# Attention and routed experts in fp32 on one core: whole loads of q, k and v, a new order of the work, and copies in place of the last pair's last moves

## The chip, the core and the metric

The kernel runs on one core of one Trainium2 chip. The metric is device time in microseconds: the median of three runs was 614.49 us (614.11 to 616.44). Five engines take part: TensorE (PE), VectorE (DVE), ScalarE (ACT), GpSimd (POOL) and SyncE (SP), which only issues DMAs.

## What is computed

For 8 batches of 8 heads, 576 positions and head size 64, attention with rotary embedding; then, per batch, the 128 positions with the highest gate score go through a small expert network, and its result is added to their rows.

```python
scores = scale * np.matmul(q_rot, k_rot.transpose(0, 1, 3, 2))
scores = scores - np.max(scores, axis=-1, keepdims=True)
attn = np.exp(scores)
attn = attn / (np.sum(attn, axis=-1, keepdims=True) + 1e-09)
x = np.matmul(attn, v)                      # heads side by side: 8 x 576 x 512
scores = np.einsum('bsd,d->bs', x, w_gate)
top_idx = np.argpartition(-scores[b], capacity)[:capacity]
h = np.maximum(x[b, top_idx] @ w1, 0.0)
out[b, top_idx] = x[b, top_idx] + sigmoid(scores[b, top_idx])[:, None] * (h @ w2)
```

## The kernel before

**Pairs and units.** The 64 heads are worked in 32 pairs, four pairs to a batch. Inputs come packed by the host. For a pair, `load` brings k, q and v: k and q as two DMAs each, one for each half of the 128 partitions (line 464), v as one DMA to partitions 0 to 63 (line 456), which an ACT or POOL copy doubles into partitions 64 to 127 (line 459). `rotate` makes the rotary sums on POOL (lines 482, 484) and splits them into a high and a low part (lines 486, 487). `attend` makes nine units of 128 query rows: three PE products (line 536), the row maxima on DVE (line 557), the exponentials on ACT (line 565), and a 32 by 32 block transpose on DVE into `pt` (line 588). Units 0 to 3 go to `pt0`, units 4 to 8 to `pt1`.

**Moves.** After the block transposes, quarters of 32 partitions must change places. Half of what must move is first set aside by an ACT or POOL copy (line 594). Then `move` issues four DMAs from SBUF to SBUF (line 610): two `gone` moves, and two more that wait for the first two. Only then can `value` multiply by v (line 635; 128 columns for `pt0`, 160 for `pt1`), copy out (lines 347, 349), transpose back (line 688) and scale rows (lines 703 to 719). The row sums of unit 8 are spread over partitions by four small POOL copies (line 670).

**Routing and the expert.** After a batch's fourth pair, `route` makes gate scores (774), spreads them (784), counts for each row how many are higher (793, 801 to 807), and selects 128 rows (841, 849). POOL gathers these rows from the output in DRAM with an indirect DMA (865). PE transposes them (883), and the expert runs as PE products in chunks (911) with transposes of the hidden layer between (930). DVE adds the result (946), and POOL scatters it back (950). The expert of batch 6 is held until the end of the last batch.

**What sets the order.** Every piece is an `op` with the engines it may run on, an estimated cost, a priority key and what it needs. `Order.run` is a planner that walks through simulated time and gives each free engine the ready op with the smallest key; the engines then run that order as it stands, each strictly in order, with semaphores between them. Keys come from the table `KEY` (20000 units are a pair) plus noise drawn from `SEEDS`, one seed for each pair's stretch. Where PE has nothing to do in the plan and has lately been little busy, the planner puts in a filler: a product whose result nobody reads (line 358). `op`s that may run on two engines are given to the one that is free.

Of the kernel before, what the change touches and what calls it, by code (L numbers as in the profile page):

```python
# [19 lines left out]
P = 128  # L20
# [3 lines left out]
KEY = dict(warm=0.7, warm0=20000, warm1=1000000, dummy=430, dcols=256, ahead=12000, lag=16000, rem=400, value=10000, rows=3000, load=26000, rotate=115700, half=2500,  # L24
           gate=11700, route=58400, count=35500, select=12400, turn=17500, step=7600, kstep=2700, hold=3,
           vcopy=3000, lift=range(9), lifted=740, patience=900, over=300, near=-300, swap=6000, vsplit=9, vstep=0, recip=6000, pool_lo=1, esplit=2, t_most=4)


SEEDS = (85, 648, 427, 874, 17, 496, 720, 7, 849, 752, 45, 62, 610, 72, 955, 819, 905, 1, 133, 973, 819, 418, 418, 526,
         36, 895, 308, 381, 162, 522, 372, 129, 880)  # L30
# [14 lines left out]
class Order:  # L45
# [33 lines left out]
    def run(self):  # L79
# [59 lines left out]
        while events:  # L139
# [3 lines left out]
            moved = True  # L143
            while moved:
                moved = False
                for e in names:
# [126 lines left out]
def attention_moe_kernel(ctx: ExitStack, tc: tile.TileContext, q, k, v, gate, w1, w2, rope, outs, shape, cap):  # L273
# [69 lines left out]
    LOAD, VALUES, WEIGHTS, STORE = {"SP": (540, 1850)}, {"SP": (500, 2050)}, {"SP": (520, 1400)}, {"SP": (600, 2200)}  # L343
# [104 lines left out]
    def load(pi, names="kqv", after=()):  # L448
# [3 lines left out]
        for i, (n, src, tiles) in enumerate((("k", k, k_ins), ("q", q, q_ins), ("v", v, vts))):  # L452
            if n in names:
                use = uses[n] = tiles.next()
                if n == "v":
                    o = op(VALUES, lambda src=src, use=use: nc.sync.dma_start(use.tile[0:64], src[b, j]), key + i,
                           use.before + list(after), size=1450)
                    y = op({"ACT": act(2 * (NB // 2) * D), "POOL": pool_copy(2 * (NB // 2) * D)},
                           lambda e, use=use: (nc.gpsimd.tensor_copy if e == "POOL" else nc.scalar.copy)(use.tile[64:P], use.tile[0:64]),
                           key + KEY["vcopy"], [o])  # L460
                    got[n] += [o, y]
                for h in range(2 if n != "v" else 0):
                    hp = slice(64 * h, 64 * h + 64)
                    o = op(LOAD, lambda src=src, use=use, hp=hp: nc.sync.dma_start(use.tile[hp], src[b, j][hp]), key + i,
                           use.before + list(after), size=1500)
                    got[n].append(o)
                use.by(*got[n])
# [44 lines left out]
    def attend(pi):  # L512
# [36 lines left out]
        def softmax(u, key, o, b):  # L549
# [12 lines left out]
            m = op({"DVE": (KEY["lifted"], KEY["lifted"] + 131) if lift else (665, 796)}, most, key,  # L562
                   [o] + nm.before + (into.before if lift else []), b, urgent=True)
            x = op({"ACT": (728, 838)},
# [12 lines left out]
        def turn(u, key):  # L577
# [19 lines left out]
            area[c].by(o, y), side_[c].by(y)  # L597
            return [o, y]

        def move(c, key, turns):  # L600
# [15 lines left out]
            turns = sum(turns, [])  # L616
            gone = {g: part(g, two[e, 1], two[o_, 0], turns) for g, (e, o_) in up.items()}
# [8 lines left out]
        def value(c, key):  # L626
            acc, ot = Bank("s"), ots[c].next()

            def products(m0, m1):
                for m in range(m0, m1):  # L630
                    for h in range(2):
                        for g in range(2):
# [4 lines left out]
                                vt.tile[gp_, h, (m - 1) % 2 * NT + (m - 1) // 2 if m else 2 * NT, :],  # L637
# [26 lines left out]
        def reciprocals(key):  # L664

            def spread():
                for h in range(2):
                    for a in range(2):
                        at_ = 64 * a + 32 * h
                        nc.gpsimd.tensor_copy(su[32 * a:32 * a + 32, 8 + h, 0:1], su[at_:at_ + 32, 10, 0:1])  # L670
# [5 lines left out]
            sp = op({"POOL": (870, 945)}, spread, key, exps[8])  # L676
# [87 lines left out]
    def route(b):  # L764
        base = at(NP * b + NP - 1, 1.0) + KEY["route"]
        last = b == B - 1
        gp, done, stored, rs = gates.pop(b)
# [11 lines left out]
        after = key + (0 if last else KEY["count"])  # L779
# [328 lines left out]
```

## Time and profile before

| | us |
|---|---|
| median of three runs (range) | 614.49 (614.11 to 616.44) |
| the profiled execution | 613.23 |
| its span, first to last instruction | 611.4 |
| around the span | 1.8 |
| PE, DVE, ACT, POOL busy | 547.9, 496.5, 459.1, 458.3 |

The profile is of one execution. Busy time is the sum of the instructions' spans on an engine; PE's is modelled, since matmuls are pipelined, and it holds the fillers too. An idle time is put down to what ended it. In the chain of waits, the last instruction is followed back, step by step, to what released it.

### The profile page before, as it was taken

The numbers are of one execution on the slowest core, as the hardware profiler recorded it, in microseconds if no ns is written. First come the engines' busy times: TensorE is split into PE (matmuls) and PEld (weight loads), VectorE is DVE, ScalarE is ACT, GpSimd is POOL, SyncE is SP. The second block draws the span as 40 slices with busy tenths as digits, with TensorE's granted clock in tenths as the row PEclk, the third lists the DMA queues.
The fourth block names the chain that finished last, engine by engine and source line by source line (L and its number), as shares of the span: only waits on it lengthen the run. The fifth ranks groups of instructions, "written<-read, shape, count | busy, mean of one in ns | idle before, by whom it ended". The sixth has DMA issues, their size and how long they took to land.

```text
span 611.4 us, 19675 instructions
## 1 busy us (share of the span) xinstructions
PE 547.9 (90%) x7570; PEld 451.5 (74%) x7570; DVE 496.5 (81%) x1248; ACT 459.1 (75%) x1201; POOL 458.3 (75%) x479
## 2 busy tenths in 40 slices
PE   0887989996999998999989999899989999899996
PEld 0675767785887787788868787778878887688874
DVE  4978878895899999898989889889988999788221
ACT  2768899896788888788788868878789877776411
POOL 1889999997888788898878788788898698622110
PEclk9988999999899999999989999999999999899999
DMA  8599999889688698979887787877888776626410
GB/s 204 120 221 223 215 247 229 205 201 240 137 183 206 167 229 199 229 171 221 197 231 162 158 233 177 201 167 210 197 232 193 180 198 152 178 65 156 116 35 17
DMA packets 55166, 111.59 MB, mean 183 GB/s; under 512 B 7840, under 2 KB 37536, under 8 KB 55072
## 3 DMA queue, kind: packets, MB, share of 16 engines
q1 hardware_dynamic: 53648, 105.42, 72.0%
q0 software_dynamic: 1280, 4.20, 2.4%
q8 instruction: 59, 0.97, 0.7%
q10 hardware_dynamic: 144, 0.72, 0.4%
q14 instruction: 35, 0.29, 0.2%
HBM read 56.30 MB, written 11.53 MB: 111 GB/s over the span
## 4 chain that ended last, share of the span: by engine, by line
PE 33%; DMA 26%; POOL 14%; issue 10%; DVE 7%; ACT 6%; SPq 3%; POOLq 0%; DVEq 0%; ACTq 0%
DMA pt<-pt 11%; PE ps L635 11%; PE ps L911 9%; PE ps L536 9%; DMA xe<-out_dram,idx 6%; POOL turned L484 3%; DVE pab L557 3%; DMA vt<-v_dram 3%; ACT pab L565 2%; PE ps L688 2%; DVE pt L588 2%; POOL q_in L482 2%; DMA h<-w_dram 2%; POOL w L977 2%; POOL k_in L482 2%
## 5 line engine op out<-in xcount | busy, mean ns | idle before, releaser
L565 ACT ACTIVATE pab<-pab,nm 128x576 f32<-128x576 f32 x256 | 196.6, 770 | 34.5 <-DVE pab L557 33.4
L557 DVE TENSOR_SCALAR_CACHE_REDUCE pab<-ps 128x576 f32<-128x576 f32 x256 | 181.5, 745 | 35.7 <-PE ps L536 30.5
L588 DVE STREAM_TRANSPOSE pt<-pab 128x576 f32<-128x576 f32 x256 | 188.6, 760 | 21.4 <-ACT pab L565 20.9
L635 PE MATMUL ps<-pt,vt 64*64 64x128 f32 (+1 forms) x4608 | 165.6, 291 | 8.4 <-DMA pt<-pt 2.6
L635 PEld LDWEIGHTS ps<-pt,vt 64*64 64x64 f32 x4608 | 146.2, 136 | 25.0 <-issue 8.9
L536 PE MATMUL ps<-kh,qh 64*128 64x288 f32 (+1 forms) x576 | 89.7, 351 | 22.7 <-ACT qh L486 15.1
L482 POOL TENSOR_TENSOR q_in<-q_in,tabs 128x1280 f32<-128x1280 f32 x31 | 91.1, 2940 | 22.2 <-DMA q_in<-q_dram 21.9
L594 ACT COPY pt<-pt 128x288 f32<-128x288 f32 x223 | 88.6, 429 | 23.3 <-DMA pt<-pt 7.8
L536 PEld LDWEIGHTS ps<-kh,qh 64*128 64x128 f32 (+1 forms) x576 | 51.2, 190 | 59.6 <-issue 19.6
L482 POOL TENSOR_TENSOR k_in<-k_in,tabs 128x1152 f32<-128x1152 f32 x31 | 82.7, 2666 | 2.4 <-DMA k_in<-k_dram 2.2
L536 PE MATMUL ps<-kh,ql 64*128 64x288 f32 (+1 forms) x576 | 71.7, 299 | 2.7 <-POOL ql L487 2.6
L536 PE MATMUL ps<-kl,qh 64*128 64x288 f32 (+1 forms) x576 | 70.9, 296 | 0.0
L688 PE MATMUL ps<-turner,ot 128*128 128x136 f32 x320 | 52.4, 295 | 8.0 <-ACT ot L347 7.1
L358 PE MATMUL ps<-tabs,turner 128*128 128x256 f32 x202 | 56.3, 402 | 1.3 <-DVE pab L557 0.9
L536 PEld LDWEIGHTS ps<-kh,ql 64*128 64x128 f32 (+1 forms) x576 | 53.9, 190 | 3.6 <-POOL ql L487 3.0
L688 PEld LDWEIGHTS ps<-turner,ot 128*128 128x128 f32 x320 | 42.7, 191 | 16.7 <-ACT ot L347 11.0
L536 PEld LDWEIGHTS ps<-kl,qh 64*128 64x128 f32 (+1 forms) x576 | 54.0, 190 | 0.0
L487 POOL TENSOR_TENSOR ql<-turned,qh 128x640 fp32r<-128x640 f32 x31 | 48.4, 1562 | 6.3 <-ACT qh L486 5.3
L911 PE MATMUL ps<-w,ht 128*128 128x512 f32 x192 | 51.6, 408 | 0.0
L911 PE MATMUL ps<-w,xt 128*128 128x512 f32 x192 | 51.3, 407 | 0.0
L594 POOL COPY pt<-pt 128x288 f32<-128x288 f32 x65 | 27.3, 427 | 29.1 <-DVE pt L588 13.5
L484 POOL TENSOR_TENSOR turned<-q_in 128x640 f32<-128x640 f32 x31 | 48.3, 1558 | 1.1
(104 smaller groups left out, 769.1 us busy)
## 6 DMA issues: line engine op xcount, KB each, us to landing
pt<-pt SPq DMA_DIRECT2D x128, 180.0 KB
q_in<-q_dram SPq DMA_DIRECT2D x64, 320.0 KB
k_in<-k_dram SPq DMA_DIRECT2D x64, 288.0 KB
pt<-pt SPq DMA_DIRECT2D x128, 144.0 KB
vt<-v_dram SPq DMA_DIRECT2D x32, 288.0 KB
out_dram<-x SPq DMA_DIRECT2D x16, 512.0 KB
xe<-w_dram SPq DMA_DIRECT2D x8, 256.0 KB
h<-w_dram SPq DMA_DIRECT2D x8, 256.0 KB
```

Of the source, the lines that this page charges most:

```text
L358: nc.tensor.matmul(bank_of(b)[:, 0:KEY["dcols"]], ident, tabs[:, 0, 0:KEY["dcols"]], start=True, stop=True)
L482: m = op(time(2 * n), lambda: e.tensor_tensor(x[:, :, c0:c1], x[:, :, c0:c1], tab[:, :, c0:c1], op=ALU.mult), key, got)
L484: y = op(time(n), lambda: e.tensor_tensor(sum_[:, c0:c1], x[:, 0, c0:c1], x[:, 1, c0:c1], op=ALU.add), key, [m] + sum_use.before)
L487: d = op(time(n), lambda: e.tensor_tensor(lu.tile[:, c0:c1], sum_[:, c0:c1], hu.tile[:, c0:c1].bitcast(F32), op=ALU.subtract), base, [c] + ...
L536: nc.tensor.matmul(bank_of(bs[i])[:, n, 0:HALF], lt, rt, start=start, stop=stop)
L557: nc.vector.tensor_scalar(halves, bank_of(b)[:, :, 0:HALF], -1.0, None, op0=ALU.mult, op1=ALU.min, accum_out=nm.tile[:, u:u + 1])
L565: lambda: nc.scalar.activation(halves, halves if lift else bank_of(b)[:, :, 0:HALF], AF.Exp, bias=nm.tile[:, u:u + 1], scale=-1.0 if lift ...
L588: nc.vector.transpose(into, src.rearrange("p (m w j) -> p m w j", w=2, j=32))
L594: (nc.gpsimd.tensor_copy if e == "POOL" else nc.scalar.copy)(apart(c)[:, to * L:to * L + L], two)
L635: nc.tensor.matmul(bank_of(acc)[64 * h:64 * h + 64, g, c0:c0 + 32 * n], vt.tile[gp_, h, (m - 1) % 2 * NT + (m - 1) // 2 if m else 2 * NT, ...
L688: nc.tensor.matmul(bank_of(b)[:, W * i:W * i + W], ot.tile[:, i * P:i * P + P], turner, start=True, stop=True)
L911: nc.tensor.matmul(bank_of(bank), lhs.tile[:, a, c * P:c * P + P], w[w_][:, c, fs], start=(c == 0 and i == 0), stop=(c == n - 1 and i == 2))
```

## The change

- `load`: k and q are one DMA each over 128 partitions. v is repacked by the host so that one DMA brings 576 elements to each of 128 partitions, and two copies of 64 partitions by 576 elements put each half beside the other; `value` picks its operand accordingly.
- `move` and `turn`: for the `pt1` side of the last pair, the four DMAs are left out. Instead each of the five block transposes is followed by four copies of 32 partitions by 288 elements on ACT or POOL.
- the spread of unit 8's row sums may also run on ACT.
- the planner: an op on PE that needs only another op on PE is ready as soon as PE is free, not when the first one's result has landed; the expert's products are cut into chunks of one (`esplit` 1, before 2), so that a chunk is three matmuls.
- the keys, seeds and some estimated costs are new; batch 6 has its own keys for counting, selecting and turning.

```diff
-           gate=11700, route=58400, count=35500, select=12400, turn=17500, step=7600, kstep=2700, hold=3,
+           gate=10237, route=58400, count=31062, select=10850, turn=21875, step=7600, count_=20000, select_=3000, turn_=78750, step_=8550, last_step=1750, kstep=2700, hold=3,
...
-                        n.ready = max(n.ready, o.end + self.SEM)
+                        behind = e == "PE" and "PE" in n.engines
+                        n.ready = max(n.ready, free[e] if behind else o.end + self.SEM)
...
-                    o = op(VALUES, lambda src=src, use=use: nc.sync.dma_start(use.tile[0:64], src[b, j]), key + i,
-                    y = op({"ACT": act(2 * (NB // 2) * D), "POOL": pool_copy(2 * (NB // 2) * D)},
+                    o = op(VALUES, lambda src=src, use=use: nc.sync.dma_start(use.tile[:, 0], src[b, j]), key + i,
+                    for h in range(2):
+                        mine, there = slice(64 * h, 64 * h + 64), slice(64 - 64 * h, 128 - 64 * h)
+                        got[n].append(op({"ACT": act((NB // 2) * D), "POOL": pool_copy((NB // 2) * D)},
+                                             use.tile[mine, 1], use.tile[there, 0]), key + KEY["vcopy"], [o]))
-                for h in range(2 if n != "v" else 0):
-                    o = op(LOAD, lambda src=src, use=use, hp=hp: nc.sync.dma_start(use.tile[hp], src[b, j][hp]), key + i,
+                    got[n].append(op(LOAD, lambda src=src, use=use: nc.sync.dma_start(use.tile, src[b, j]), key + i,
...
+            if not c or pi < n_pairs - 1:
+                return [o, y]
+            for g in (0, 2):
+                e, o_ = slice(32 * g, 32 * g + 32), slice(32 * g + 32, 32 * g + 64)
+                needs = [o, y]
+                for out, in_ in ((two[e], one[o_]), (one[o_], apart(c)[e, to * L:to * L + L])):
+                    needs = [op({"ACT": act(L, 30), "POOL": pool_copy(L)},
...
+            if c and pi == n_pairs - 1:
+                return
...
-            sp = op({"POOL": (870, 945)}, spread, key, exps[8])
+            sp = op({"ACT": (340, 440), "POOL": (870, 945)}, spread, key, exps[8])
```

The order that comes out differs on every engine. Three places follow; the number behind a tile's name is its buffer's.

**PE, batch 4, from the selection to the transposes of the gathered rows.** L849 is the last selection product, L883 the transposes of the gathered rows; L536 are score products, L635 the products with v, L688 transposes back, L358 fillers. Before:

```order
L849 MATMUL ps<-tok_114,more 128x5
L635 MATMUL ps<-pt_91,vt_86 64x128 x36
L358 MATMUL ps<-tabs,turner 128x256
L536 MATMUL ps<-kh_79,qh_83 128x288 x4
L536 MATMUL ps<-kl_81,qh_83 128x288 x4
L536 MATMUL ps<-kh_79,ql_85 128x288 x4
L688 MATMUL ps<-turner,ot_93 128x136 x2
L358 MATMUL ps<-tabs,turner 128x256 x2
L536 MATMUL ps<-kh_79,qh_83 128x288 x4
L536 MATMUL ps<-kl_81,qh_83 128x288 x4
L536 MATMUL ps<-kh_79,ql_85 128x288 x4
L883 MATMUL ps<-turner,xe_109 128x128 x4
```

Now, with other line numbers (L897 are the transposes of the gathered rows); ahead of these rows and behind the selection stand two transposes back and a block of 36 products with v from `pt1`:

```order
L537 MATMUL ps<-kh_79,qh_83 128x288 x4
L537 MATMUL ps<-kl_81,qh_83 128x288 x4
L537 MATMUL ps<-kh_79,ql_85 128x288 x4
L537 MATMUL ps<-kh_79,qh_83 128x288 x2
L537 MATMUL ps<-kl_81,qh_83 128x288 x2
L537 MATMUL ps<-kh_79,ql_85 128x288 x2
L701 MATMUL ps<-turner,ot_94 128x136 x3
L537 MATMUL ps<-kh_79,qh_83 128x288 x4
L537 MATMUL ps<-kl_81,qh_83 128x288 x4
L537 MATMUL ps<-kh_79,ql_85 128x288 x4
L648 MATMUL ps<-pt_91,vt_86 64x128 x36
L897 MATMUL ps<-turner,xe_109 128x128 x4
```

Between the selection and these transposes there now stand two blocks of products with v instead of one, thirty score matmuls instead of twenty-four, and no filler instead of three.

**POOL, the end of the last pair.** L950 is the scatter of batch 5's expert, L865 the gather for batch 6, L594 the copies aside. Before:

```order
L594 COPY pt_92<-pt_92 128x288 x3
L594 COPY pt_91<-pt_91 128x288 x3
L594 COPY pt_92<-pt_92 128x288 x2
L950 DMA out_dram<-xe_109,idx_113 576x512
L864 CAST idx_112<-gg_116 128x1
L865 DMA xe_109<-out_dram,idx_112 128x512
```

Now (L606 are the new copies, L964 the scatter, L879 the gather):

```order
L595 COPY pt_92<-pt_92 128x288
L606 COPY pt_92<-pt_92 32x288 x5
L595 COPY pt_92<-pt_92 128x288
L606 COPY pt_92<-pt_92 32x288 x2
L964 DMA out_dram<-xe_109,idx_113 576x512
L606 COPY pt_92<-pt_92 32x288 x8
L878 CAST idx_112<-gg_116 128x1
L879 DMA xe_109<-out_dram,idx_112 128x512
```

Fifteen of the twenty new copies are POOL's, eight of them behind the scatter and ahead of the gather; five are ACT's. On SP the last four moves of `pt_92` are gone.

**PE, the last expert (batch 7), from its first product to its second.** L911 are the expert's products, L930 transposes of the hidden layer. Before:

```order
L911 MATMUL ps<-w_0_118,xt_106 128x512 x2
L911 MATMUL ps<-w_1_119,xt_106 128x512
L911 MATMUL ps<-w_0_118,xt_106 128x512
L930 MATMUL ps<-turner,h_108 128x128 x8
L358 MATMUL ps<-tabs,turner 128x256 x2
L911 MATMUL ps<-w_0_120,ht_107 128x512
```

Now (L925 the products, L944 the transposes):

```order
L944 MATMUL ps<-turner,h_108 128x128 x4
L925 MATMUL ps<-w_0_118,xt_106 128x512
L925 MATMUL ps<-w_1_119,xt_106 128x512
L925 MATMUL ps<-w_0_118,xt_106 128x512 x2
L925 MATMUL ps<-w_1_119,xt_106 128x512
L925 MATMUL ps<-w_0_118,xt_106 128x512
L925 MATMUL ps<-w_0_120,ht_107 128x512
L925 MATMUL ps<-w_1_121,ht_107 128x512
L925 MATMUL ps<-w_0_120,ht_107 128x512
L944 MATMUL ps<-turner,h_108 128x128 x4
L925 MATMUL ps<-w_0_120,ht_107 128x512
```

The first four transposes now stand after 18 of the 24 products of the first layer, and three products of the second layer stand ahead of the last four transposes. The six last products of batch 6's expert now stand behind the transposes of batch 7's gathered rows, where they stood ahead of them.

## Rows read from the trace of the kernel before

**Rows 1.** The page: TensorE's and the other engines' busy time, and the clock.

```profile
PE 547.9 (90%) x7570; PEld 451.5 (74%) x7570; DVE 496.5 (81%) x1248; ACT 459.1 (75%) x1201; POOL 458.3 (75%) x479
...
core 0: 611.4 us, clock 0.980
```

**Rows 2.** The page: the chain that ended last, shares of the span by engine.

```profile
PE 33%; DMA 26%; POOL 14%; issue 10%; DVE 7%; ACT 6%; SPq 3%; POOLq 0%; DVEq 0%; ACTq 0%
```

**Rows 3.** Stretches: us, busy us by engine, granted clock, DMA share, GB/s.

```profile
40.00:140.00 100.00, 89.77 (x1293) 73.27 (x1290) 85.39 (x210) 88.82 (x235) 96.56 (x90) 0.98 0.93 219
85.00:515.00 430.00, 400.43 (x5817) 332.11 (x5818) 378.89 (x951) 353.03 (x925) 366.00 (x368) 0.98 0.82 197
```

**Rows 4.** Waits over the whole span: total us, times, longest us.

```profile
PE ps L883 <- DMA xe<-out_dram,idx: 13.8, 6, 4.1
...
POOL sums L670 <- DMA xe<-out_dram,idx: 8.3, 3, 3.9
```

**Rows 5.** Instructions in time: PE's transposes of gathered rows, batches 0, 1 and 5.

```profile
150.88 1.12 PE L883 MATMUL ps<-turner,xe 128*128 128x128 f32 x4 [4.08 <-DMA xe<-out_dram,idx]
...
250.76 0.66 PE L883 MATMUL ps<-turner,xe 128*128 128x128 f32 x4 [1.05 <-DMA xe<-out_dram,idx]
...
524.18 0.66 PE L883 MATMUL ps<-turner,xe 128*128 128x128 f32 x4 [2.77 <-DMA xe<-out_dram,idx]
```

**Rows 6.** Stretches behind three of these transposes, columns as in rows 3.

```profile
151.00:158.00 7.00, 7.00 (x89) 5.93 (x90) 4.19 (x10) 3.11 (x7) 5.13 (x6) 0.58 0.37 82
317.50:321.00 3.50, 3.47 (x15) 2.63 (x17) 0.89 (x4) 2.32 (x6) 1.90 (x7) 0.53 0.84 216
524.00:531.00 7.00, 6.82 (x94) 5.83 (x95) 4.17 (x12) 5.48 (x14) 5.52 (x9) 0.76 0.46 138
```

**Rows 7.** Groups of instructions (count, busy us, mean ns, idle before): the fillers.

```profile
L358 PE MATMUL ps<-tabs,turner 128*128 128x256 f32 x202 | 56.3, 402 | 1.3 <-DVE pab L557 0.9 <-DMA pt<-pt 0.4
```

**Rows 8.** Instructions in time: PE's two last blocks with v, two fillers.

```profile
566.60 2.20 PE L635 MATMUL ps<-pt,vt 64*64 64x128 f32 x72
...
569.86 1.03 PE L358 MATMUL ps<-tabs,turner 128*128 128x256 f32 x4
571.22 3.12 PE L635 MATMUL ps<-pt,vt 64*64 64x160 f32 x72 [0.33 <-issue]
```

**Rows 9.** Stretches near the start, columns as in rows 3.

```profile
3.00:5.00 2.00, 0.00 (x0) 0.00 (x0) 0.12 (x5) 0.00 (x0) 0.00 (x0) 1.00 1.06 312
5.00:12.00 7.00, 0.00 (x0) 0.00 (x0) 2.11 (x2) 0.66 (x1) 0.00 (x0) 1.00 1.00 215
17.00:18.00 1.00, 1.00 (x12) 1.00 (x12) 0.73 (x2) 0.00 (x0) 0.48 (x1) 1.00 0.83 271
```

**Rows 10.** The chain in order of time: first and last of six loads, one unit pair's scores.

```profile
1.47 7.57 DMA k_in<-k_dram
...
391.23 0.99 PE ps L536 x12
...
481.08 7.27 DMA q_in<-q_dram
```

**Rows 11.** Groups of instructions: the copies that the change splits, moves or resembles.

```profile
L459 ACT COPY vt<-vt 64x1152 f32<-64x1152 f32 x24 | 27.7, 1153 | 9.0 <-DMA vt<-v_dram 8.5
L486 ACT CAST kh<-turned 128x576 fp32r<-128x576 f32 x32 | 21.4, 670 | 14.1 <-DVE turned L484 8.8 <-POOL turned L484 4.6 <-PE ps L536 0.6
L594 POOL COPY pt<-pt 128x288 f32<-128x288 f32 x65 | 27.3, 427 | 29.1 <-DVE pt L588 13.5 <-DMA pt<-pt 10.7 <-DVE rs L673 4.0
L705 ACT COPY gp<-ps 128x4 f32<-128x4 f32 (+1 forms) x26 | 4.4, 170 | 0.0
L670 POOL COPY sums<-sums 32x1 f32<-32x1 f32 x128 | 22.8, 178 | 19.9 <-DMA xe<-out_dram,idx 8.3 <-ACT pr L565 7.7
L793 DVE SCALAR_TENSOR_TENSOR more<-ps,sc,above 128x320 bf16<-128x320 f32 (+4 forms) x40 | 20.0, 535 | 1.0 <-PE ps L784 1.0
```

**Rows 12.** Instructions in time: the last pair's last maximum and copy aside, the last expert.

```profile
560.85 0.09 DVE L557 DVE_READ_ACCUMULATOR pab<-ps 128x1 f32 x1
...
564.03 0.43 ACT L594 COPY pt<-pt 128x288 f32<-128x288 f32 x1 [0.83 <-DVE xe L946]
...
591.62 6.12 PE L911 MATMUL ps<-w,xt 128*128 128x512 f32 x24
...
597.58 0.60 PE L930 MATMUL ps<-turner,h 128*128 128x128 f32 x4
...
600.10 5.94 PE L911 MATMUL ps<-w,ht 128*128 128x512 f32 x24
```

**Rows 13.** DMA issues: gathers and scatters, median us from issue to landing.

```profile
xe<-out_dram,idx POOLq DMA_INDIRECT x7, 6.5
out_dram<-xe,idx POOLq DMA_INDIRECT x7, 3.2
```

More of the change, by code (lines that the diff above doesn't have):

```diff
@@ L560, in most @@
                     nc.vector.tensor_reduce(nm.tile[:, u:u + 1], bank_of(b)[:, :, 0:HALF], axis=AX.XY, op=ALU.max, negate=True)
-            m = op({"DVE": (KEY["lifted"], KEY["lifted"] + 131) if lift else (665, 796)}, most, key,
+            m = op({"DVE": (KEY["lifted"], KEY["lifted"] + 75) if lift else (665, 796)}, most, key,
                    [o] + nm.before + (into.before if lift else []), b, urgent=True)
-            x = op({"ACT": (728, 838)},
+            x = op({"ACT": (768, 870) if lift else (728, 838)},
                    lambda: nc.scalar.activation(
@@ L597, in turn @@
             area[c].by(o, y), side_[c].by(y)
+            if not c or pi < n_pairs - 1:
[5 more added lines that the diff above has]
+                    needs = [op({"ACT": act(L, 30), "POOL": pool_copy(L)},
+                                lambda e, out=out, in_=in_: (nc.gpsimd.tensor_copy if e == "POOL" else nc.scalar.copy)(out, in_),
+                                key, needs)]
+                    area[c].by(*needs), side_[c].by(*needs), moved[c].extend(needs)
             return [o, y]
@@ L664, in reciprocals, with spread @@
         def reciprocals(key):
-            def spread():
+            def spread(e):
                 for h in range(2):
@@ L669, in spread @@
                         at_ = 64 * a + 32 * h
-                        nc.gpsimd.tensor_copy(su[32 * a:32 * a + 32, 8 + h, 0:1], su[at_:at_ + 32, 10, 0:1])
+                        (nc.gpsimd.tensor_copy if e == "POOL" else nc.scalar.copy)(su[32 * a:32 * a + 32, 8 + h, 0:1], su[at_:at_ + 32, 10, 0:1])
             def f():
@@ L766, in route @@
         last = b == B - 1
+        K = {n: KEY[n + "_" * (b == B - 2)] for n in ("count", "select", "turn", "step")}
         gp, done, stored, rs = gates.pop(b)
@@ L778, in route @@
         split = splits(sc, s, key)
-        after = key + (0 if last else KEY["count"])
+        after = key + (0 if last else K["count"])
         scores = lambda t: bank_of(bs).rearrange("p n c -> p (n c)")[0:P if t < NT else REM, t * P:S]
@@ L810, in route @@
         sc.by(s, o, *counts), mores.by(co), cnt.by(*counts, co)
-        return [chosen(b, r0, base + (0 if last else KEY["count"] + KEY["select"]), bc, co, stored, split, last)
+        return [chosen(b, r0, base + (0 if last else K["count"] + K["select"]), bc, co, stored, split, last, K)
                 for r0 in range(0, cap, P)]
@@ L827, in splits, with chosen @@
         return tk, o
-    def chosen(b, r0, key, bc, co, stored, split, last):
+    def chosen(b, r0, key, bc, co, stored, split, last, K):
         n = min(P, cap - r0)
@@ L860, in index @@
                 nc.vector.memset(xe.tile, 0.0)
-        ix = op({"DVE": dve(2, 2, 600.0 * (n < P))}, index, key, [w] + xe.before + gg.before, bp)
+        ix = op({"DVE": dve(2, 2, 600.0 * (n < P))}, index, key, [w] + (xe.before if n < P else []) + gg.before, bp)
         def rows_in():
@@ L871, in chosen, with experts_of @@
         idx.by(ga)
[L872 to L874 removed]
+        return lambda hold: experts_of(b, n, key, last, K, ga, ix, idx, xe, gg, hold)
+    def experts_of(b, n, key, last, K, ga, ix, idx, xe, gg, hold):
         xt, ht = xts.next(), hts.next()
         g = gg.tile
[L877 to L878 removed]
+        step = KEY["last_step"] if last else K["step"]
+        key += 0 if last else K["turn"]
         bx = Bank("t")
```

28 lines of the change are left out of this document (11 added, 17 removed).

## The prediction

> **What bounds the kernel now.** I read the busy shares first. PE is busy for 547.9 of 611.4 us, DVE for 496.5, ACT for 459.1, POOL for 458.3 [rows 1]: no engine is full, and PE's number holds 202 filler records, 56.3 us [rows 7], that compute nothing. The reader should see that the useful work of PE is 547.9 - 56.3 = 491.6 us, and that DVE has as much. The chain of waits says the same: PE is a third of it, DMAs are 26% [rows 2], so the end is set by a relay in which each engine in turn is late. In the middle stretch, from 85 to 515 us, PE is busy 93%, DVE 88%, POOL 85%, ACT 82% [rows 3]. Only the early stretch, in which the expert's weights are loaded too, is close to full somewhere: POOL 97%, DMA share 0.93 from 40 to 140 us [rows 3].
>
> So what counts is where the fixed orders make an engine stand in front of something late. The list of waits names one such place plainly: PE stands before the transposes of the gathered rows (L883) for 13.8 us in six batches, 4.1 us at worst [rows 4, 5]. The median gather takes 6.5 us from issue to landing [rows 13]. [...]
>
> **Part 1, the new order around the gathers.** In batches 0, 2, 3, 4 and 5 the old order puts one block of products with v between the selection and L883, the new one two. A block lasts 2.2 to 3.1 us [rows 8]; thirty score matmuls stand where 24 did in batch 4 (0.99 us for twelve [rows 10]), and three fillers, half of 1.03 us each [rows 8], are gone. In batch 4 the second block is of the longer kind, so the work that covers the gather grows by about 3.1 + 0.5 - 1.5 = 2.1 us, and by three transposes back. Batch 1 goes the other way: two blocks before and after, but twelve score matmuls fewer, so its wait of 1.05 us [rows 5] may grow by 1 us. Upper bound of the gain: 13.8 - 1.05 = 12.7 us of waiting and 6.3 us of clock, 19 us. Lower bound: nothing, if the other engines have used the pause to catch up. A second bound comes from the orders: the new one has 64 fillers, the old one 101, and a filler stands only where the plan had nothing for PE. At 56.3 / 101 = 0.56 us each [rows 7] the 37 fewer are 20.6 us. Both ends agree on some 20 us, and I take somewhat under half, **-9 us**, since DVE at 88% [rows 3] has only an eighth of its time to give.
>
> POOL also stops at a gather: a row-sum copy waits until the DMA lands, 8.3 us in three batches [rows 4]. In the new order such a wait still stands behind each gather or scatter (behind batch 3's gather it stands before a v copy). I count no gain here.
>
> **Part 2, whole loads.** Sixty-four issues fall away on SP, which costs nothing to the end by itself, as the moves behind them mostly wait for data. The bytes are the same. Near the start 312 GB/s flow while the 128-partition table is in flight and 215 while mainly halves are [rows 9]; but for one microsecond, with only the two halves of q in flight, 271 [rows 9]. Six loads are on the chain, from 7.57 us for the first k to 7.27 us for a late q, 35 us in all [rows 10]. If all sped up as 215 to 312, they would be 31% shorter: -11 us, one end. The other end is 0, since a chain that loses a load finds the next wait. By the nearest row, 271 to 312, it is 13% of 35 = 4.6 us; I take **-3 us**, the first load's part included.
>
> [...]
>
> v's copy is split. One ACT copy of 1152 elements takes 1.153 us, an ACT cast of 576 elements 0.670 [rows 11]; two are 1.34 us, 0.19 more, but they may run on two engines and start after a shorter load. I take 0.
>
> **Part 3, row sums on ACT.** By the order, 84 of the 128 small copies move from POOL to ACT. The smallest ACT copy takes 0.170 us [rows 11], so ACT gets 14.3 us, and 15.0 us leave POOL (0.178 each [rows 11]). With v's copies (45 x 0.670 - 27.7 = 2.5) and nine copies aside or moves (3.9 at POOL's 0.427 [rows 11]) ACT has 20.7 us more. The cover is ACT's idle time, 430 - 353 = 77 us in the middle stretch [rows 3]. If that cover is gone, all 20.7 us are paid. I take **+1 us**.
>
> **Part 4, the last pair's moves.** Now the last copy aside ends at 564.46 [rows 12], and the last block with v starts at 571.22 [rows 8]: 6.8 us for four moves in two steps. After it, each transposed unit is followed by four copies, 0.43 us each [rows 11]. Even if POOL did all four of the last unit in a row, that is 1.7 us: up to 5.1 us gained. Two things take some back. On DVE five counting operations for batch 6, 0.535 us on average [rows 11], now stand between the last maxima and the last two transposes: 2.7 us, partly where DVE would wait for ACT anyway. And on POOL eight of the copies stand behind batch 5's scatter, and the second of them waits for its landing, 3.2 us [rows 13]. The scatter's sum stands earlier on DVE than before, ahead of the last maxima, so the landing should be over in time. If not, the gain is about 0. I take **-3 us**.
>
> **Part 5, the last expert.** The first layer's products end at 591.62 + 6.12 = 597.74, the second layer's start at 600.10 [rows 12]: 2.36 us, of which two sets of transposes need 1.2. In the new order six products of the first layer and three of the second fill these gaps. **-1 us**, with bounds 0 and -1.2 here, and up to 1 us more because batch 6's last six products cover the conversion of batch 7's rows.
>
> **The sum.** -9 - 3 + 1 - 3 - 1 = -15 us. The profiled execution took 613.23 us (span 611.4 and 1.8 around it), so 598.2; it lies 1.26 us under the median of the runs, so on that scale I say **599 us**.
>
> **Rivals.**
>
> *Another engine keeps the pace.* PE no longer waits for gathers, but DVE, at 88%, and the relay through ACT do not deliver more scores or exponentials, and PE's pause only moves to L536 or L635. For it: the middle stretch has no single bound [rows 3]. Against: three of the waits cost the clock as well [rows 6]. Part 1 is then 0 and the sum -6: 608.5 us.
>
> *The waits go in full.* Part 1 is worth its 19 us and loads half of their upper end, 5.5 us: -19 - 5.5 - 3 - 1 = -28.5, 586 us.
>
> *ACT becomes late.* The spread of row sums stands in ACT's strict queue behind the exponential of unit 8, and the next exponentials stand behind it. If these copies are on the path of each pair, as when ACT is past about 95% in a stretch (it has 89% from 40 to 140 us [rows 3]), half to all of the 20.7 us is paid, and part 1 does not show: +10.4 or +20.7, less 7 for parts 2, 4 and 5, so +3 to +14 and in the middle 613.2 + 8.5 + 1.3 = 623 us, slower than before.
>
> *The clock falls instead.* Where fillers went, PE may pause more. Each fall costs 1.6 to 2.9 us [rows 6]. If the waits at the gathers stay and every batch has two more such falls of 1.6 us, that is 26 us against the -7 of parts 2, 4 and 5 (and +1 for ACT): about 633 us; with one in each batch, 13 us, 620. It decides once falls number more than four beyond today's. [...]
>
> **How the numbers follow.** The forecast (592 to 606 by its bounds) has a chance of 0.60, another engine keeping the pace 0.20 (its range 605 to 614), the waits going in full 0.08, ACT late 0.06, the clock 0.06. A measurement here can tell about 0.5%, 3 us, from no change: below 611.4 is faster, above 617.6 slower. Faster holds the forecast, the full case and most of the second: 0.60 + 0.08 + 0.13 = 0.81. Same gets the rest of the second and a little of the slower cases, 0.09; slower 0.10. The range leaves out about 2 in 10: the slower cases above, half of the full case below: 588 to 613.
>
> **What would show it.** [...] Wrong: PE waiting as long at the gather, or for maxima in its place; ACT's idle share vanishing with DVE waiting for it; POOL's new copies standing idle before the scatter's landing; more clock falls than now.

## The result and the profile after

The changed kernel takes **586.16 us** (median of four runs, 585.07 to 593.77), the kernel before 615.47 beside it (614.11 to 616.59): a ratio of 0.955, 95% interval 0.947 to 0.964. The sign is as forecast, the time is not: 599 was said, with a range of 588 to 613. The profiled execution took 585.07 us, its span is 583.3.

The page of the changed kernel: busy times, one DMA queue, and the chain's shares by engine.

```profile
PE 523.4 (90%) x7496; PEld 434.2 (74%) x7496; DVE 495.5 (85%) x1242; ACT 477.9 (82%) x1318; POOL 452.9 (78%) x417
...
q1 hardware_dynamic: 53968, 104.67, 65.4%
...
DMA 28%; ACT 22%; POOL 17%; PE 10%; issue 10%; DVE 9%; SPq 2%; POOLq 0%; ACTq 0%; DVEq 0%
```

Beside [rows 1, 2]: PE's share of the chain fell from 33% to 10%, and ACT's rose from 6% to 22%. ACT has 18.8 us more work, nearly the 20.7 of part 3, and the end came sooner all the same. The kernel before has this row for the same queue, which carries all loads and moves (the last number is the time that its packets took, as a share of the 16 DMA engines' span):

```profile
q1 hardware_dynamic: 53648, 105.42, 72.0%
```

72.0% of 611.4 us is 440 us on each of the 16 engines; 65.4% of 583.3 is 381. The bytes are within 1%. So **59 us of DMA time are gone, and the bytes are not**. This row of before was not among those that the prediction was built on, and it should have been.

The waits of the changed kernel over the whole span, columns as in [rows 4]:

```profile
DVE pt L589 <- ACT pab L566: 33.2, 47, 2.0
POOL q_in L483 <- DMA q_in<-q_dram: 23.2, 17, 4.4
...
ACT pab L566 <- DVE pab L558: 7.0, 17, 1.2
DVE pab L558 <- PE ps L537: 6.1, 7, 3.6
...
PE ps L897 <- DMA xe<-out_dram,idx: 0.9, 1, 0.9
...
POOL sums L683 <- DMA out_dram<-xe,idx: 0.4, 1, 0.4
```

PE's wait for the gather was 13.8 us [rows 4] and is 0.9. The kernel before has these two rows:

```profile
DVE pab L557 <- PE ps L536: 30.5, 26, 5.4
...
DVE pt L588 <- ACT pab L565: 20.9, 31, 2.4
```

DVE's wait for scores is down from 30.5 us in 26 places to 6.1 in 7: PE is hardly late any more. DVE's wait for ACT's exponentials is up, from 20.9 to 33.2. The stretches, columns as in [rows 3], and the fillers:

```profile
3.00:5.00 2.00, 0.00 (x0) 0.00 (x0) 0.12 (x5) 0.00 (x0) 0.00 (x0) 1.00 0.98 376
5.00:12.00 7.00, 0.00 (x0) 0.00 (x0) 4.56 (x6) 1.34 (x2) 2.02 (x2) 1.00 0.76 291
40.00:140.00 100.00, 89.59 (x1331) 74.37 (x1329) 86.64 (x214) 93.25 (x253) 92.66 (x66) 0.97 0.80 225
85.00:515.00 430.00, 402.99 (x6062) 334.30 (x6061) 391.57 (x985) 383.81 (x1069) 368.48 (x325) 1.00 0.76 206
```

```profile
L359 PE MATMUL ps<-tabs,turner 128*128 128x256 f32 x128 | 35.7, 403 | 2.6 <-POOL pt L595 1.4 <-ACT gp L718 1.2
```

The start runs at 376 and 291 GB/s, where it was 312 and 215 [rows 9], and from 5 to 12 us with a DMA share of 0.76 instead of 1.00. The DMA share from 85 to 515 us is 0.76 (0.82 in [rows 3]) at more GB/s, the granted clock there 1.00 instead of 0.98, and 128 filler records are left of 202.

**Where the time went.** Each pair has one sum for its reciprocals, on DVE (line 673 before, 686 now). Pairs 21 and 22 in the kernel before, then in the changed one; PE's transposes of batch 3's gathered rows stand between:

```profile
374.39 0.12 DVE L673 TENSOR_REDUCE rs<-sums 128x10 f32<-128x20 f32 x1
394.48 0.15 DVE L673 TENSOR_REDUCE rs<-sums 128x10 f32<-128x20 f32 x1
```

```profile
358.22 0.13 DVE L686 TENSOR_REDUCE rs<-sums 128x10 f32<-128x20 f32 x1
374.14 0.17 DVE L686 TENSOR_REDUCE rs<-sums 128x10 f32<-128x20 f32 x1
```

That step is 20.1 us before and 15.9 now. Thirty-two such starts cut a span into the time to the first, 31 steps, and the rest. In before, the transposes of gathered rows lie in the steps to pairs 8, 14, 18, 22, 26 and 30, the gather pairs; in the changed kernel the first has gone to pair 10 (a step of 17.8 us, pair 8's is 17.7), the others are where they were. Summed from these records, in us (the runs below the first two are the experiments' profiled executions):

| | to the first | six gather pairs | 25 other steps | rest | span |
|---|---|---|---|---|---|
| before | 30.9 | 121.9 | 411.2 | 47.5 | 611.4 |
| after | 30.1 | 96.6 | 411.8 | 44.9 | 583.3 |
| before's order, whole loads | 31.2 | 115.3 | 403.9 | 48.4 | 598.8 |
| before's order, no gather wait | 31.4 | 106.2 | 416.6 | 47.5 | 601.7 |
| after's order, half loads | 31.6 | 95.8 | 433.8 | 44.3 | 605.6 |
| after, routing keys of before | 29.9 | 100.1 | 421.2 | 53.0 | 604.2 |

So 25.3 of the 28 us come out of the six gather pairs. That looks as if the gathers were the whole story; the experiments say otherwise. (Between two orders the table can't tell a gain from work that moved to a neighbour; within one order it can.)

### The profile page after: what moved, and what is told of

It reads as the page before. It is cut to its first block, busy times and chain, and to the rows that moved or that the text cites. A ratio compares the mean times of both kernels' runs of the same rounds, so it can differ in the third digit from the quotient of the medians.

```text
span 583.3 us, 19385 instructions
## 1 busy us (share of the span) xinstructions
PE 523.4 (90%) x7496; PEld 434.2 (74%) x7496; DVE 495.5 (85%) x1242; ACT 477.9 (82%) x1318; POOL 452.9 (78%) x417
## 3 DMA queue, kind: packets, MB, share of 16 engines
q1 hardware_dynamic: 53968, 104.67, 65.4%
## 4 chain that ended last, share of the span: by engine, by line
DMA 28%; ACT 22%; POOL 17%; PE 10%; issue 10%; DVE 9%; SPq 2%; POOLq 0%; ACTq 0%; DVEq 0%
DMA pt<-pt 11%; ACT pab L566 8%; DMA q_in<-q_dram 7%; DMA vt<-v_dram 6%; ACT pt L595 4%; PE ps L648 4%; POOL turned L485 4%; POOL q_in L483 4%; DVE pt L589 4%; POOL k_in L483 3%; DVE pab L558 3%; PE ps L537 2%; ACT vt L463 2%; POOL kl L488 2%; PE ps L925 2%
## 5 line engine op out<-in xcount | busy, mean ns | idle before, releaser
L589 DVE STREAM_TRANSPOSE pt<-pab 128x576 f32<-128x576 f32 x256 | 190.3, 762 | 36.4 <-ACT pab L566 33.2
L648 PE MATMUL ps<-pt,vt 64*64 64x128 f32 (+1 forms) x4608 | 159.3, 286 | 6.4 <-DVE pab L558 3.6
L648 PEld LDWEIGHTS ps<-pt,vt 64*64 64x64 f32 x4608 | 141.3, 133 | 18.9 <-issue 5.5
L537 PE MATMUL ps<-kh,qh 64*128 64x288 f32 (+1 forms) x576 | 90.0, 350 | 31.2 <-ACT qh L487 15.0
L595 ACT COPY pt<-pt 128x288 f32<-128x288 f32 x227 | 89.9, 429 | 16.9 <-DMA pt<-pt 8.4
L925 PE MATMUL ps<-w,xt 128*128 128x512 f32 x192 | 52.9, 409 | 0.0
L925 PE MATMUL ps<-w,ht 128*128 128x512 f32 x192 | 51.1, 405 | 0.0
L566 ACT ACTIVATION_READ_ACCUMULATOR pab<-pab,nm 128x1 f32 x256 | 48.2, 188 | 0.0
L488 POOL TENSOR_TENSOR kl<-turned,kh 128x576 fp32r<-128x576 f32 x31 | 44.1, 1423 | 2.4 <-ACT kh L487 2.1
```

The costliest lines, as they stand in the source:

```text
L488: d = op(time(n), lambda: e.tensor_tensor(lu.tile[:, c0:c1], sum_[:, c0:c1], hu.tile[:, c0:c1].bitcast(F32), op=ALU.subtract), base, [c] + ...
L537: nc.tensor.matmul(bank_of(bs[i])[:, n, 0:HALF], lt, rt, start=start, stop=stop)
L566: lambda: nc.scalar.activation(halves, halves if lift else bank_of(b)[:, :, 0:HALF], AF.Exp, bias=nm.tile[:, u:u + 1], scale=-1.0 if lift ...
L589: nc.vector.transpose(into, src.rearrange("p (m w j) -> p m w j", w=2, j=32))
L595: (nc.gpsimd.tensor_copy if e == "POOL" else nc.scalar.copy)(apart(c)[:, to * L:to * L + L], two)
L648: nc.tensor.matmul(bank_of(acc)[64 * h:64 * h + 64, g, c0:c0 + 32 * n], vt.tile[gp_, h ^ g, (m - 1) % 2 * NT + (m - 1) // 2 if m else 2 * ...
```

## The experiments

The expectations name their theories by letters. G: PE's stop at the gathers is most of the gain (part 1). L: the whole loads are most of it, so far more than the 3 us of part 2. P: the row sums taken off POOL are most of it (part 3). Two more are about the loads alone. R: a transfer over half the partitions moves slowly. I: the second issue and the second transfer cost the time. Every ratio is to the kernel before on the same chip, with its 95% interval; differences in us are of medians, and what is said "by the interval" or "by the ratio" is worked out from the ratio of some 614 us.

### Each part alone, in the order of before

**b_no_gather_wait**, the wait at L883 taken away (the transposes read the rotary table, so the expert's input is left out):

```diff
-  nc.tensor.transpose(bank_of(bx)[:, c * P:c * P + P], xe.tile[:, c * P:c * P + P], ident)
+  nc.tensor.transpose(bank_of(bx)[:, c * P:c * P + P], tabs[:, 0, c * P:c * P + P], ident)
```

> The kernel before, in its own order, but PE's transposes ahead of each expert read the rotary table instead of the gathered rows, so that PE waits for no gather (the expert's input is left out of what is computed; the gather itself and the scatter stay). [...] Theory L (the whole loads are most of it) and theory P (the row sums taken off POOL are most of it): under 8 us, 608 us or more.

Measured: 604.08 us, 0.986 (0.978 to 0.995), **-10 us**, 3 to 14 by the interval. Part 1 had taken -9 from a bound of 19. For theory G the author had expected 594 to 602 us: the time is 2 us above that, and well below 608. In the table, 15.7 us leave the gather pairs and 5.4 come back in the others.

**b_whole_loads**, part 2 alone (v's two copies, the operand of `value` and the host's packing go with it, and are not shown):

```diff
-  nc.sync.dma_start(use.tile[0:64], src[b, j])
+  nc.sync.dma_start(use.tile[:, 0], src[b, j])
...
-  nc.sync.dma_start(use.tile[hp], src[b, j][hp])
+  None if h else nc.sync.dma_start(use.tile, src[b, j])
```

> The kernel before, in its own order, but k and q as one DMA each over 128 partitions at the place of the first half, and v as 576 elements to each of 128 partitions with two copies of 64 x 576 on the engine that made the one copy. Theory L: 595 to 604 us. Theories G and P: within 4 us of before, 611 to 616 us, as loads are on the chain for 35 us and lose 13% at the nearest row.

Measured: 601.60 us, 0.981 (0.973 to 0.989), **-13 us**, 7 to 17 by the interval, where part 2 took -3 and its bound was -11. That is theory L's range. The queue, the start and the chain by line:

```profile
q1 hardware_dynamic: 54672, 105.41, 62.9%
```

```profile
3.00:5.00 2.00, 0.00 (x0) 0.00 (x0) 0.12 (x5) 0.00 (x0) 0.00 (x0) 1.00 0.97 384
5.00:12.00 7.00, 0.00 (x0) 0.00 (x0) 4.00 (x5) 2.01 (x3) 1.74 (x2) 1.00 0.77 297
```

```profile
PE ps L636 8%; PE ps L537 7%; DMA xe<-out_dram,idx 6%; DMA pt<-pt 6%; PE ps L912 5%; DVE pab L558 5%; POOL turned L485 4%; DVE pt L589 4%; POOL q_in L483 4%; ACT pab L566 4%; POOL k_in L483 4%; POOL kl L488 2%; POOL ql L488 2%; DMA k_in<-k_dram 2%; DMA q_in<-q_dram 2%
```

62.9% of 598.8 us is 377 us on each DMA engine, 63 less than before, 2 us for each pair. The chain's loads went from six with 35.1 us to five with 32.4: hardly less. The moves, which share the queue, have 6% of the chain (`DMA pt<-pt`), 11% before. The chain shows little of what changed. The rows below are POOL's wait for q, before and here, and PE's wait for the gather here:

```profile
POOL q_in L482 <- DMA q_in<-q_dram: 21.9, 14, 2.6
```

```profile
POOL q_in L483 <- DMA q_in<-q_dram: 6.3, 7, 1.4
...
PE ps L884 <- DMA xe<-out_dram,idx: 9.3, 5, 3.0
```

Summed over the lists of waits, PE, DVE, ACT and POOL stand 20 us in front of loads, 54 before; in front of moves 17 instead of 21. PE's wait for the gather is 9.3 us instead of 13.8, so whole loads take a part of that loss away too.

**b_whole_no_wait**, both of these edits.

> The kernel before, in its own order, with both of its edits that paid: whole loads, and transposes that read the rotary table instead of the gathered rows (the expert's input is left out of what is computed). If the two gains are apart (13 and 10 us), 589 to 593 us. If they are one and the same slack, 598 to 602 us.

Measured: 591.34 us, 0.963 (0.952 to 0.974) of 617.75: -26 us, 16 to 30 by the interval. The -10 and -13 **add up** within the noise: for the most part they are two separate losses. One and the same slack would have been 598 us or more.

**b_sums_on_act**, the row sums of unit 8 by ACT instead of POOL, all of them:

```diff
-  nc.gpsimd.tensor_copy(su[32 * a:32 * a + 32, 8 + h, 0:1], su[at_:at_ + 32, 10, 0:1])
+  nc.scalar.copy(su[32 * a:32 * a + 32, 8 + h, 0:1], su[at_:at_ + 32, 10, 0:1])
```

> The kernel before, in its own order, but the four small copies that spread unit 8's row sums run on ACT instead of POOL, which also takes away POOL's stops for the landing of gathers and scatters at these copies. Theory P: 600 to 606 us. Theory G: 608 to 618 us, since PE still stands before the gathered rows; ACT gets 128 copies of some 0.17 us, 22 us, beside 77 us and more of idle time.

Measured: 613.62 us, 0.998 (0.994 to 1.002). No effect that shows: in this order the work is hidden on either engine, and POOL's stop at the gather's landing (8.3 us, [rows 4]) cost nothing either.

### The loads, in the order of after

**a_half_loads** (k, q and v over halves, v doubled by two copies), **a_kq_by_halves** (k and q alone, two DMAs of 64 partitions), **a_kq_by_columns** (as many DMAs, but each over 128 partitions and half the columns), **a_v_by_half** (v alone). The lines for k and q:

```diff
-  nc.sync.dma_start(use.tile, src[b, j])
+  [nc.sync.dma_start(use.tile[64 * h:64 * h + 64], src[b, j][64 * h:64 * h + 64]) for h in range(2)]   # halves
+  [nc.sync.dma_start(use.tile[:, h], src[b, j][:, h]) for h in range(2)]                               # columns
```

> The changed kernel, in its own order, but each load of k and q issued as two DMAs over 64 partitions back to back, and v brought to partitions 0 to 63 and doubled by the same two copies. Theory L: the gain goes back by 10 us or more, 596 to 605 us. Theories G and P: 586 to 591 us.

> The changed kernel, in its own order, but only k and q over partition halves; v stays over 128 partitions. By bytes, k and q are 1216 of the 1504 KB that a pair loads, so of the 22 us some 18 should come back under theory R: 600 to 606 us. Theory I: the same number, as the issues are all here.

> The changed kernel, in its own order, but each load of k and q issued as two DMAs, each over all 128 partitions and half the columns; as many issues and the same bytes as the halves of before. Theory R (what costs is how fast a transfer over half the partitions moves): within 4 us of the changed kernel, 586 to 590 us. Theory I (what costs is a second issue on SP and a second transfer in the rings): most of the 22 us of the half loads come back, 600 us or more.

> The changed kernel, in its own order, but only v brought to partitions 0 to 63, in one DMA as now, and doubled by the same two copies. Theory R: by bytes 4 us come back, or more, since v is alone over half of the partitions and has no second half beside it: 589 to 596 us. Theory I: nothing, 586 to 588 us, as the number of issues is the same.

| | us | ratio to before (95%) | queue q1, share | us on each engine |
|---|---|---|---|---|
| changed kernel, as above | 586.16 | 0.955 (0.947 to 0.964) | 65.4% | 381 |
| a_half_loads | 608.57 | 0.992 (0.988 to 0.996) | 72.8% | 441 |
| a_kq_by_halves | 606.43 | 0.987 (0.976 to 0.999) | 71.4% | 432 |
| a_v_by_half | 591.22 | 0.962 (0.952 to 0.972) | 66.5% | 393 |
| a_kq_by_columns | 580.66 | 0.946 (0.936 to 0.956) | 64.9% | 375 |

Two DMAs over halves cost some 20 us over the changed kernel and 26 over two DMAs by columns, which ran on the same chip; the columns cost nothing. It is **the half of the partitions, not the number of issues**: theory R, not I. Two of these runs lie clearly outside their ranges all the same: a_half_loads is 4 us above its own, a_kq_by_columns 5 below. v alone, at 0.962, is not clear of the changed kernel's repeats below. The stretch near the start and the chain by line of a_half_loads:

```profile
5.00:12.00 7.00, 0.00 (x0) 0.00 (x0) 2.57 (x4) 0.67 (x1) 0.00 (x0) 1.00 0.98 215
```

```profile
DMA pt<-pt 10%; DMA k_in<-k_dram 8%; DMA vt<-v_dram 7%; ACT pab L566 6%; PE ps L648 6%; DMA q_in<-q_dram 5%; POOL turned L485 4%; DVE pt L589 3%; ACT pt L595 3%; DVE pab L558 3%; SPq L621 3%; POOL k_in L483 3%; PE ps L537 3%; SPq L466 2%; POOL kl L488 2%
```

Again 215 GB/s at a share of 0.98. And with halves in the new order **21 loads stand on the chain, 122 us**, the first and the last of them below (start and length, us); the changed kernel has 13 with 75 us, the kernel before six with 35 [rows 10].

```profile
2.73 8.72 DMA q_in<-q_dram
...
517.45 5.71 DMA q_in<-q_dram
```

The table of steps shows where. With half loads the new order has its gather pairs as short as with whole ones (95.8 and 96.6 us), but the 25 other steps are 22.0 us longer: that is where late loads cost. Put together, as ratios to before:

| | loads in halves | whole loads |
|---|---|---|
| order of before | 1 | 0.981 |
| new order, with parts 3 to 5 | 0.992 | 0.955 |

By these ratios of some 614 us, whole loads are worth 12 in the old order and 22 in the new; the new order is worth 5 with half loads and 16 with whole ones. One by one they give 17 us, together 28. The changed kernel's repeats below have 0.963 and 0.956; with these it is 18 to 22, 11 to 16, and 23 to 28 together. So **each seems to lift the other**, but with intervals of 2 to 7 us on each ratio this is not far from the noise.

### Is anything left of the gather waits?

**a_no_gather_wait**, the first edit in the order of after.

> The changed kernel, in its own order, with the transposes reading the rotary table instead of the gathered rows (the expert's input is left out of what is computed). If the new order already covers the gathers, nothing changes: within 2 us of the changed kernel. If gathers still cost time, as on POOL's stops: 2 to 6 us less.

Measured: 588.03 us, 0.963 (0.954 to 0.972), beside 588.52 for **after_again**, the changed kernel on the same chip. Nothing measurable is left to take. Batch 0 shows why, from the gather's issue to PE's transposes:

```profile
159.54 1.25 POOL L879 DMA_INDIRECT xe<-out_dram,idx  x1 [0.29 <-POOL idx L878]
...
161.65 2.68 PE L648 MATMUL ps<-pt,vt 64*64 64x160 f32 x72
...
165.25 2.19 PE L648 MATMUL ps<-pt,vt 64*64 64x128 f32 x72
...
169.25 0.66 PE L897 MATMUL ps<-turner,xe 128*128 128x128 f32 x4
```

9.7 us lie between, with the two blocks of products with v that the order promised, and no wait is marked on the last row, where 4.08 us stood [rows 5].

### The order by itself

**a_old_priorities**: the changed code with keys and seeds of before.

> The changed kernel's code with the keys and seeds of the kernel before (the new keys set to the old ones' values). The whole loads stay, so under the finding of the earlier runs the 13 us that they give in the old order stay too, and what the new priorities give at the gathers goes: 598 to 606 us, with PE standing 8 us or more before the gathered rows. If the order's density in general is what the new seeds gave, more: 606 to 614 us.

Measured: 620.81 us, 1.016 (1.007 to 1.026). Both ranges missed. With the loads whole it should have been near 601; the new code under the old keys is some 10 us *slower* than before, by the ratio.

**a_old_route_keys** puts back the keys of routing and expert alone; **old_new_route_keys** has all keys of before but these:

```diff
-  gate=10237, ..., count=31062, select=10850, turn=21875, step=7600, count_=20000, select_=3000, turn_=78750, step_=8550, last_step=1750
+  gate=11700, ..., count=35500, select=12400, turn=17500, step=7600, count_=35500, select_=12400, turn_=17500, step_=7600, last_step=100
```

> The changed kernel with the keys for routing and the expert (gate, count, select, turn, step and the new ones of batch 6 and the last expert) as before; all other keys and the seeds are new. If the distance at the gathers is what the keys gave, PE stands 8 us or more before the gathered rows again and 10 us or more come back: 598 us or more. If the other keys carry it: 587 to 594 us.

> The changed code with the old keys and seeds, but the keys for routing and the expert new. If that group carries the 32 us: 590 to 605 us. If the others do: 612 to 622 us.

Measured: 606.74 us (0.992, 0.987 to 0.997) and 620.69 us (1.014, 1.003 to 1.025). Taking the routing keys back costs 20 us, giving them alone brings nothing. So the keys work only together. The time came back as the first range said, but its reason did not: PE's wait for the gather stays away with the old routing keys. What returns in part is DVE's wait for scores, 16.0 us where it was 6.1:

```profile
DVE pab L558 <- PE ps L537: 16.0, 22, 3.3
...
PE ps L897 <- DMA xe<-out_dram,idx: 0.7, 1, 0.7
```

By the table of steps, of 21 us in the span 8.1 are in the rest after the last pair, 9.4 in the other steps and 3.5 in the gather pairs. So to have whole loads and no gather wait is not enough for 586 us. Why the new code is slow under the old keys is open; the planner's new rule and the new costs, which are in that code, were not tried alone, nor the new keys on the old code.

**a_other_seeds** and **b_other_seeds** draw other noise for the keys:

> The changed kernel with every seed of the noise on the keys raised by a constant, so that only the draw differs. If the drawn order is worth much by itself: 598 to 612 us. If the loads and the keys carry the gain: 586 to 594 us.

> The kernel before with its seeds raised in the same way. If the drawn order is worth much by itself: 626 to 645 us. If not: 611 to 620 us.

Measured: 588.96 us (0.965, 0.954 to 0.976) beside 586.02 for **after_third** on the same chip, and 620.93 us (1.017, 1.006 to 1.029) beside before's 614.85. The other draw costs some 3 us in the changed kernel and 6 to 10 in the kernel before, whose 620.93 lies between its two ranges. With these draws too the two kernels are 32 us apart, so the gain is hardly luck of the draw; one more draw of each was tried.

### The last pair's moves

**a_moves_by_dma**: the changed kernel with the last four moves as DMAs again; the planner places the end anew.

```diff
-  if not c or pi < n_pairs - 1:
+  if True:
     return [o, y]
```

> The changed kernel with the last pair's last moves as four DMAs again, as before; the planner places the end anew, all the rest stands as it was. By the prediction 3 us come back, up to 5: 588 to 591 us. If the landing of the scatter already ate the gain: within 1 us of the changed kernel.

Measured: 590.83 us, 0.967 (0.958 to 0.976), 2.3 more than after_again, though the runs of the two overlap (589.08 to 592.17, 584.14 to 592.33). First here, then in the changed kernel, the last maximum and the last blocks with v (the row at 541.87 holds two blocks, 128 and 160 columns; the block for `pt1`, of 160, starts at 543.89):

```profile
538.94 0.09 DVE L558 DVE_READ_ACCUMULATOR pab<-ps 128x1 f32 x1
...
551.86 2.79 PE L647 MATMUL ps<-pt,vt 64*64 64x160 f32 x72
```

```profile
535.38 0.08 DVE L558 DVE_READ_ACCUMULATOR pab<-ps 128x1 f32 x1
535.43 1.06 POOL L964 DMA_INDIRECT out_dram<-xe,idx  x1 [0.28 <-POOL pt L606]
...
540.79 3.27 POOL L606 COPY pt<-pt 32x288 f32<-32x288 f32 x7 [3.83 <-DMA out_dram<-xe,idx]
541.87 4.89 PE L648 MATMUL ps<-pt,vt 64*64 64x128 f32 x144
...
543.89 0.59 PE L648 MATMUL ps<-pt,vt 64*64 64x160 f32 x10
...
544.88 1.06 POOL L879 DMA_INDIRECT xe<-out_dram,idx  x1 [0.57 <-POOL idx L878]
```

The last block starts 8.4 us after the last maximum instead of 12.8. Of these 4.4 us 0.8 are given back: behind the block's start 39.4 us pass to the end, and 38.6 with the DMAs. So 3.6 us are left in these two executions. The feared wait came: seven of POOL's copies stood 3.83 us for the scatter's landing and ended at 544.06, about when the last block starts, with the gather of batch 6 behind them. What it cost was not tried.

### Two more runs of what was best

> The changed kernel itself, on the same chip as these runs, to compare with: 585 to 589 us.

> The changed kernel itself, to compare with on this chip: 585 to 589 us.

> The changed kernel with k and q as two DMAs each by columns over all partitions, again, on the same chip as the changed kernel. If this is a faster version: 579 to 583 us, 4 us or more below the changed kernel. If it was the chip: within 2 us of it.

Measured: the changed kernel 588.52 and 586.02 us; k and q by columns 581.64 us, 0.951 (0.942 to 0.960), after 580.66 the first time. On the chip where both ran, the runs are 581.17 to 583.86 by columns and 582.62 to 589.57 for the changed kernel. So two DMAs by columns, each over all partitions, are the **best version of this study, some 4 to 5 us under the changed kernel**, though the runs overlap a little. The loads land sooner after their issue (KB each, median us). By columns, then the changed kernel:

```profile
q_in<-q_dram SPq DMA_DIRECT2D x64, 320.0 KB, 4.9
k_in<-k_dram SPq DMA_DIRECT2D x64, 288.0 KB, 4.2
```

```profile
q_in<-q_dram SPq DMA_DIRECT2D x32, 640.0 KB, 5.6
k_in<-k_dram SPq DMA_DIRECT2D x32, 576.0 KB, 6.0
```

The second issue comes 0.4 us after the first. Why two are better than one was not settled.

## Why the prediction was right and wrong

**Faster: right, and the two reasons named are shown in the old order.** Half loads and gather waits each have an edit of their own, and with both edits the old order has 0.963 of before, where the changed kernel has 0.955 to 0.963. How the new keys come to the same is shown only in part.

**Part 1, -9: right in size where it was tested.** The waits alone are worth 10 us in the old order; the new one leaves 0.9 of 13.8, and the stretch from 85 to 515 us has the clock at 1.00. What the new order gives with parts 3 to 5 seems to depend on the loads, 5 us with half loads and 11 to 16 with whole ones, and a sum of independent parts could not say so. The 6.3 us of clock in its upper bound are an estimate from [rows 6]: 0.42 x 7, 0.47 x 3.5 and 0.24 x 7 us, what the granted clock of 0.58, 0.53 and 0.76 leaves of those stretches. No run shows them apart from the waits; with the waits taken away the kernel is 10 us faster in all. Nor is the wait its whole account: with the old routing keys PE waits 0.7 us for the gather, and the kernel takes 606.74 us.

**Part 2, -3: here the prediction failed.** The mechanism stands, its size does not: 12 us in the old order, 18 to 22 in the new. Two choices made it small. The first was the price, 271 against 312 GB/s from one microsecond, taken as nearest because both halves of a load were in flight. That microsecond is the fastest of its load: from 16 to 20 us the two halves of q have 72, 271, 236 and 77 GB/s. Where the DMA engines are full they move 236, and the whole load of q in the changed kernel moves 389 (before, then after):

```profile
18.00:19.00 1.00, 1.00 (x9) 0.72 (x8) 1.00 (x5) 0.76 (x2) 1.00 (x1) 1.00 1.03 236
```

```profile
18.00:19.00 1.00, 1.00 (x9) 0.72 (x7) 1.00 (x5) 0.65 (x1) 0.00 (x0) 1.00 0.97 389
```

Over the run, halves cost 60 us of DMA time on each engine, in a_half_loads too, and the 7 us at 215 GB/s with the DMA share at 1.00 [rows 9] were the row to take: against 312 they are the 31% that the prediction kept as its far end. The second choice was the quantity: only the six loads that stood on the chain of before, 35 us. A chain names what was last in one order. The new order has 21 half loads there, 122 us, and off the chain engines stand in front of loads as well: whole loads take this idle time from 54 to 20 us in the old order and from 98 to 62 in the new. So -11 was no bound: 12 us is not clear of it, 18 to 22 lies beyond it.

Nor is it the second DMA: two halves issued back to back are 26 us slower than two DMAs by columns, each over all partitions (606.43, 580.66).

**Part 3, +1: not contradicted.** Nothing measurable in b_sums_on_act, in the old order. ACT's 18.8 us more in the changed kernel were not tried alone; ACT's larger share of the chain says that they need not be hidden there.

**Part 4, -3: agrees in size, but is not clear of the noise.** The last block starts 8.4 us after the last maxima, 10.3 before; the author had expected 6 to 8. Undoing the change costs 3.6 us from the last maximum to the end in the two executions shown, and 2.3 us by the medians, within the spread. POOL's wait at the scatter came, 3.83 us of it, where the prediction took the landing to be over in time.

**Part 5, -1: its gain is not shown.** From the last pair's reciprocals to the end 2.6 us are gained, parts 4 and 5 together (-4 was said). With the moves as DMAs again, so with part 5 alone, this stretch is 48.5 us, not shorter than the 47.5 of before. The last expert's layers do run on without a gap:

```profile
570.09 1.64 PE L925 MATMUL ps<-w,xt 128*128 128x512 f32 x6
571.57 0.86 PE L925 MATMUL ps<-w,ht 128*128 128x512 f32 x3
572.48 0.66 PE L944 MATMUL ps<-turner,h 128*128 128x128 f32 x4
572.89 5.13 PE L925 MATMUL ps<-w,ht 128*128 128x512 f32 x21
```

**The rivals.** *Another engine keeps the pace* at 608.5 has the time of the new order with half loads (608.57), by chance: late loads keep the pace there, not the relay of DVE and ACT that it named. *The waits go in full* at 586 has the measured time, but not by its sum: it put 19 us on the waits and 5.5 on the loads. *ACT late* and *the clock falls* did not come as a loss of time. The fewer loads on the chain that the author expected did not come either: 13 stand there, six before. The range's lower end stood 2 us above the time: below it lay only half of the full case, which priced the loads at 5.5 us.

## What to carry to other kernels

Read the DMA queue's own time against its bytes before pricing a load by the chain: here the DMA engines were full at 215 GB/s with half loads, where whole loads moved 291 at a share of 0.76, so it was the transfers that were slow. Take the rate from a stretch in which the engines are full, not from the one microsecond that looks nearest. A part's worth on the chain of the old order is no bound when the order changes with it. Undo each part in both orders: here the loads alone give 1.9%, the order alone 0.8%, and both 3.7 to 4.5%.

## What the runs showed of the hardware

- With k and q as two DMAs of 64 partitions each, issued back to back, the queue took 432 us of each DMA engine over the run; with two DMAs of 128 partitions and half the columns it took 375, and the kernel is 25.8 us faster (606.43, 580.66).
- The two halves of one load of q moved 236 GB/s in a microsecond with the DMA engines full, the whole load 389 (kernel before and changed kernel, 18 to 19 us).
- Two column DMAs were not slower than one whole one, but some 5 us faster (580.66 and 581.64 against 586 to 588.5), with the same bytes and 9216 more packets. The cause is open.
- By the profile, a copy on POOL behind an indirect scatter stood 3.83 us for its landing (changed kernel, 536.96 to 540.79 us) though it reads nothing of it, as the row sums had stood behind gathers (8.3 us in three, [rows 4]). What makes it wait was not tried.
